# A block-diagonal kv product, lent PSUM banks and a halved last output in a fused attention and snake-MLP kernel

## The chip, the cores and the metric

The kernel runs on one core of one Trainium2 chip. The metric is device time in microseconds (us), the median of several executions. The *span* is the time from the first to the last instruction in the profile, and the *granted clock* is the share of its full clock that TensorE was given. Engines are named as the profile names them: PE is TensorE (PEld its weight loads), DVE is VectorE, ACT is ScalarE, POOL is GpSimd, SP is SyncE. A line such as L235 is line 235 of that kernel's file, so the same statement has different numbers in different kernels.

## The reference, cut to what matters

```python
# q, k, v: (batch 8, heads 8, seq 576, head_dim 64)
q_s = softmax(q, over head_dim);  k_s = softmax(k, over seq)
kv  = einsum('bhsd,bhse->bhde', k_s, v)          # 64 x 64 for each head
x   = einsum('bhsd,bhde->bhse', q_s, kv)         # transposed and reshaped to (4608, 512)
h   = x @ w_in                                   # (4608, 2048)
g   = h + sin(alpha * h)**2 / alpha
out = g @ w_out                                  # (4608, 512)
```

The two large products are computed for nine tiles of 512 tokens ("passes" 0 to 8). A *projection* is the sixteen 128-row blocks ("slots" 0 to 15) of `h`, four 128x512 matmuls each; an *output* is 16 accumulated 128x512 matmuls for 128 tokens, four of them per tile. Attention of batch b must be done before the projection that uses its tokens.

## The kernel before

A slot's projection goes into an accumulator, a piece of PSUM (the memory that this kernel's matmuls write to; a piece of 128x512 float32 is called a *bank* here). ScalarE takes the sine, the square goes to one of three engines, and VectorE *combines* it into `g`, which frees the accumulator. (Copying an accumulator out of PSUM is called its *eviction*.) Most accumulators come from a pool of four banks, `ps_h`. Some slots use a *lent* accumulator from the pool that serves attention at that time.

```python
def mm_h(t, ni, wide=None):
    if wide and ni % 6 >= 4:            # slots 4, 5, 10, 11 are lent
        hp = wide()
    else:
        hp = ps_h.tile([128, MF], F32, name="hp", tag="h")
    for ki in range(4):                 # "..." marks what is left out, here and below
        nc.tensor.matmul(hp, win[:, ki, ...], xT[:, ki, ...], start=(ki == 0), stop=(ki == 3))
    return hp

def attn_out(b, ii, half, pool, eng):   # x of one batch: four calls, four 64x64 tiles each
    ...
    xp = pool.tile([128, 2, 512], F32, name="xp", tag="a")
    for x in range(2):
        r = slice(64 * x, 64 * x + 64)
        for e in range(2):
            nc.tensor.matmul(xp[64 * e:64 * e + 64, x, 0:n], kt[r, e, ii, :],
                             qT[r, j0:j1, ii, e * 64:(e + 1) * 64], start=True, stop=True)
    ...
    eng(xT[:, ii::2, c0:c0 + n], xp[:, :, 0:n])
```

The pool `ps_e` (two buffers of two banks) serves attention and lends in tiles 0 and 1; then it closes, and the output pool `ps_o` is laid over the same banks.

```python
with tc.tile_pool(name="ps_e", bufs=2, space=PSUM, reuse_waits="tile") as ps_e:
    def lent():
        return ps_e.tile([128, 2, MF], F32, name="hh", tag="a")[:, 0]
    ...                                  # projection 0, attention of batch 1
    for ni in range(nN):                 # projection 1
        h_slot(1, ni, SQ[ni], lag, lent)
        flush(lag, 1)                    # combine of the slot before
    cast_v(2, [GP, GP])
    flush(lag, 0)                        # combine of slot 15
ps_o = ctx.enter_context(tc.tile_pool(name="ps_o", bufs=2, space=PSUM, ...))
...
exp_q(2); exp_k(2)
os = o_stream(1)
take(os, 16)                             # first output of tile 1, and its eviction by VectorE
norm_q(2, [GP, V])                       # q reduction of batch 2, on VectorE
exp_q(3); exp_k(3); ...
q_transpose_dma(2)                       # then kv product of batch 2, then projection 2
```

The softmax here doesn't subtract the row's maximum and nothing guards it: scores larger than these inputs give would overflow.

## Time and profile before

| | before |
|---|---|
| time, median of 3 runs | 299.0 us (298.26 to 299.21) |
| span in the profile | 296.6 us |
| TensorE busy | 278.1 us, 94% |
| first projection matmul | 17.00 us |
| projection 1 starts, ends | 49.9, 63.73 us (one matmul at 49.51, the other 63 from 50.14 after a wait; 49.9 is where a start without the wait would lie) |
| projection 2 starts | 82.1 us (likewise: one matmul at 81.47, then a wait) |
| a pass of the middle (passes 3 to 6) | 30.70 us |
| last eviction starts, span ends | 291.86, 296.6 us |

The first view is the profile page of the kernel before: the busy table, then the rows of TensorE's busy share and of its granted clock over 40 slices of the span (each digit is tenths, 9 is 90% or more).

```profile
PE 278.1 (94%) x1595; PEld 127.0 (43%) x1624; DVE 185.5 (63%) x267; ACT 228.5 (77%) x320; POOL 84.6 (29%) x72
...
PE   1999998999898999999999999999999999999993
...
PEclk9999999999999999999999999999999999999999
```

TensorE bounds the kernel nearly everywhere, and every slice shows 90% or more of its clock. So anything gained must be a TensorE wait or a TensorE instruction. One caution on the clock row: the trace's clock record begins at 9.8 us here, and the row shows 9 before that only because nothing is recorded. In the timeline the fourteen warm-up matmuls show another clock:

```profile
6.29 4.90 PE L281 MATMUL warm<-qe,identb 128*128 128x512 bf16 x14 [1.99 <-ACT qe L111]
```

Most of the first nine (to 9.66 us) start 0.43 us apart, as in the half-clock stretch shown further down (67.40 to 67.83 us in the changed kernel), and the last ones (from 9.95 us) 0.22 us, as at full clock later (181.53 to 181.74 us): by this spacing the kernel starts at half clock, unseen in the row.

The second is the timeline of the kernel before around the end of projection 1, TensorE first, then VectorE. Columns: start (us), duration (us), engine, line, operation, out<-in, tile, count; in brackets the idle time before it and what ended that.

```profile
61.15 2.75 PE L215 MATMUL hp<-xT,win 128*128 128x512 bf16 x12
63.73 7.15 PE L235 MATMUL op<-wout,g 128*128 128x512 bf16 x31
...
66.24 0.75 DVE L231 SCALAR_TENSOR_TENSOR g<-s,inva_sb,hp 128x512 bf16<-128x512 f32 x1 [0.41 <-POOL s L225]
67.47 0.69 DVE L241 COPY o<-op 128x512 f32<-128x512 f32 x1 [0.48 <-PE op L235]
68.08 1.34 DVE L139 TENSOR_REDUCE qs<-qe 128x18 f32<-128x1152 bf16 x1
```

The outputs of tile 1 (L235) follow the projection (L215) without a gap, although the last combine (66.24 to 66.99) is still to come. The first output is done and evicted at 67.47, and batch 2's q reduction follows that eviction on VectorE.

The third is the timeline of one tiled attention product in a middle pass of the kernel before, and of the evictions at the very end.

```profile
182.05 0.30 PE L198 MATMUL xp<-qT,kvb 64*64 64x256 bf16 x4
182.29 0.82 PE L235 MATMUL op<-wout,g 128*128 128x512 bf16 x3
...
291.86 0.68 DVE L247 COPY o<-op 64x512 f32<-64x512 f32 x1 [2.76 <-PE op L235]
...
292.58 0.58 ACT L247 COPY o<-op 64x512 f32<-64x512 f32 x1 [14.04 <-DVE o L247]
```

The four tiles use 0.24 us of TensorE's stream (182.05 to 182.29), plus a gap of 0.10 us before them. The last output is evicted in two halves, one after the other.

The fourth is the tile view of w_in in the kernel before: the issue of its loads, and the time from issue to landing.

```profile
L101 POOL DMA_DIRECT2D win<-in_moe_w_in_dram x4: 756/765/918, 10.2 to 12.5; - x4
...
DMA to landing us min/median/max: 5.5/8.3/11.7
```

The last of four quarters was issued at 12.5 us and landed 11.7 us later, at about 24.2 us.

### The profile page before, as it was taken

The page shows a single profiled execution, that of the slowest core. Times are in us where ns is not written, and L with a number is a line of the kernel's source. Part 1 is how long each engine was busy: PE and PEld are TensorE (multiplying, and loading weights), DVE is VectorE, ACT ScalarE, POOL GpSimd, SP SyncE. Part 2 cuts the span into 40 slices and gives each one's busy share as a digit, 9 for nine tenths or more (in the row PEclk, how much of TensorE's full clock was granted, in tenths as well). Part 3 has the DMA queues.
Part 4 walks back from the last instruction along what each step waited for, and adds up shares of the span by engine and source line. Part 5 has one row for each costly group of instructions (what it writes and reads, how often), then busy time and mean ns, then how long its engine had stood idle before and what let it go on. Part 6 is the DMA issues. An engine that isn't in the chain of part 4 may idle for free.

```text
span 296.6 us, 4313 instructions
## 1 busy us (share of the span) xinstructions
PE 278.1 (94%) x1595; PEld 127.0 (43%) x1624; DVE 185.5 (63%) x267; ACT 228.5 (77%) x320; POOL 84.6 (29%) x72
## 2 busy tenths in 40 slices
PE   1999998999898999999999999999999999999993
PEld 0444454444343444344444444444444444444441
DVE  2858664889648857764786568656874555555420
ACT  4788666999577899779987998799877777777400
POOL 0949453575755635001600052005000000000000
PEclk9999999999999999999999999999999999999999
DMA  7999979966789966109921894113411111111233
GB/s 263 278 206 200 314 266 298 398 245 184 162 135 368 390 203 128 39 6 331 289 53 23 277 291 98 39 35 69 83 35 35 38 35 35 35 39 43 48 86 71
DMA packets 35540, 45.76 MB, mean 154 GB/s; under 512 B 15792, under 2 KB 20416, under 8 KB 35520
## 3 DMA queue, kind: packets, MB, share of 16 engines
q1 hardware_dynamic: 29520, 34.09, 40.8%
q0 software_dynamic: 5888, 11.27, 15.2%
q8 instruction: 12, 0.20, 0.3%
q10 hardware_dynamic: 112, 0.14, 0.2%
q14 instruction: 8, 0.07, 0.1%
HBM read 36.71 MB, written 9.44 MB: 156 GB/s over the span
## 4 chain that ended last, share of the span: by engine, by line
PE 63%; ACT 15%; DVE 8%; DMA 4%; issue 4%; POOL 3%; SPq 1%; ACTq 0%
PE hp L215 28%; PE op L235 24%; ACT s L221 4%; DVE g L231 4%; ACT ke L111 3%; DMA st_v<-in_v_dram 3%; POOL s L225 2%; PE xp L198 2%; PE acc L235 2%; PE kvp L151 2%; PE hp L235 2%; ACT s L223 2%; ACT L221 2%; ACT L111 2%; ACT qe L111 2%
## 5 line engine op out<-in xcount | busy, mean ns | idle before, releaser
L231 DVE SCALAR_TENSOR_TENSOR g<-s,inva_sb,hp 128x512 bf16<-128x512 f32 x132 | 96.8, 745 | 68.5 <-ACT s L223 54.3
L215 PE MATMUL hp<-xT,win 128*128 128x512 bf16 x515 | 130.5, 379 | 2.7 <-DVE g L231 1.2
L235 PE MATMUL op<-wout,g 128*128 128x512 bf16 x498 | 125.7, 379 | 1.2 <-issue 0.6
L221 ACT ACTIVATE s<-hp,alpha_sb 128x512 f32<-128x512 f32 x132 | 88.9, 681 | 30.4 <-PE hp L215 23.2
L215 PEld LDWEIGHTS <-win 128*128 128x128 bf16 x576 | 55.7, 98 | 70.9 <-issue 4.3
L235 PEld LDWEIGHTS <-g 128*128 128x128 bf16 x576 | 54.1, 98 | 65.4 <-DVE g L231 0.4
L223 ACT ACTIVATE s<-s 128x512 f32<-128x512 f32 x112 | 70.5, 630 | 3.7
L141 POOL TENSOR_TENSOR qn<-qe,qs 128x2304 bf16<-128x2304 bf16 (+1 forms) x8 | 26.6, 3330 | 87.2 <-DVE qs L140 81.7
L225 POOL TENSOR_TENSOR s<-s 128x512 f32<-128x512 f32 x28 | 29.5, 1061 | 23.9 <-ACT s L221 23.8
L139 DVE TENSOR_REDUCE qs<-qe 128x18 f32<-128x1152 bf16 (+1 forms) x11 | 20.7, 1882 | 14.3 <-ACT qe L111 14.2
L241 DVE COPY o<-op 128x512 f32<-128x512 f32 x31 | 21.0, 677 | 10.1 <-PE op L235 10.1
L111 ACT ACTIVATE qe<-st_q 128x1152 bf16<-128x1152 f32 x16 | 17.9, 1155 | 4.8 <-DMA st_q<-in_q_dram 4.7
L111 ACT ACTIVATE ke<-st_k 128x1152 bf16<-128x1152 f32 x16 | 17.7, 1150 | 2.6 <-DMA st_k<-in_k_dram 2.6
L201 DVE CAST xT<-xp 128x512 bf16<-128x512 f32 (+1 forms) x24 | 17.8, 747 | 1.9 <-PE xp L198 1.5
L125 POOL CAST vb<-st_v 128x1152 bf16<-128x1152 f32 x14 | 16.1, 1178 | 8.8 <-DMA st_v<-in_v_dram 8.7
L198 PE MATMUL xp<-qT,kvb 64*64 64x256 bf16 (+1 forms) x128 | 9.7, 302 | 2.7 <-DVE xT L201 1.2
L247 ACT COPY o<-op 64x512 f32<-64x512 f32 x1 | 0.6, 581 | 14.0 <-DVE o L247 14.0
L198 PEld LDWEIGHTS <-kvb 64*64 64x64 bf16 x128 | 4.5, 103 | 13.9 <-issue 11.3
L151 PE MATMUL kvp<-vb,ke 64*128 64x130 bf16 x288 | 9.8, 216 | 0.6 <-DVE qT L181 0.6
L111 ACT ACT_TABLE_LOAD x7 | 9.0, 1283 | 1.3 <-PEq L477 1.2
L151 PEld LDWEIGHTS <-ke 64*128 64x128 bf16 x288 | 8.3, 93 | 3.7 <-issue 2.4
L201 ACT CAST xT<-xp 128x640 bf16<-128x640 f32 (+1 forms) x8 | 5.1, 653 | 5.9 <-PE xp L198 5.9
(52 smaller groups left out, 112.3 us busy)
## 6 DMA issues: line engine op xcount, KB each, us to landing
out_dram<-o SPq DMA_DIRECT2D x71, 128.0 KB, 2.4
st_q<-in_q_dram SPq DMA_DIRECT2D x5, 1152.0 KB, 6.8
st_k<-in_k_dram SPq DMA_DIRECT2D x5, 1152.0 KB, 9.3
st_v<-in_v_dram SPq DMA_DIRECT2D x5, 1152.0 KB, 10.4
st_k<-in_k_dram POOLq DMA_DIRECT2D x2, 1152.0 KB, 12.2
win<-in_moe_w_in_dram POOLq DMA_DIRECT2D x4, 512.0 KB, 8.3
wout<-in_moe_w_out_dram POOLq DMA_DIRECT2D x4, 512.0 KB, 16.3
st_q<-in_q_dram SPq DMA_DIRECT2D x2, 576.0 KB, 4.8
```

The source lines that it names most:

```text
L111: nc.scalar.activation(dst[:, :, ii * 128:(ii + 1) * 128].rearrange("p j (x d) -> p x j d", x=2), src[:, ii::2], AX.Exp)
L139: nc.vector.tensor_reduce(part, src, axis=AXL.X, op=ALU.add)
L141: engs[h].tensor_tensor(dst, src, part.unsqueeze(3).to_broadcast([128, J, w, D]), op=ALU.mult)
L151: nc.tensor.matmul(kvp[:, e, ii * 130:(ii + 1) * 130], ke[r, j, ii * 128:(ii + 1) * 128], vt[r, j, ii * 130:(ii + 1) * 130], start=(j == 0 ...
L201: eng(xT[:, ii::2, c0:c0 + n], xp[:, :, 0:n])
L215: nc.tensor.matmul(hp, win[:, ki, ni * 128:(ni + 1) * 128], xT[:, ki, t * MF:(t + 1) * MF], start=(ki == 0), stop=(ki == 3))
L221: nc.scalar.activation(s, hp, AX.Sin, scale=alpha_sb[:, ni:ni + 1])
L223: nc.scalar.activation(s, s, AX.Square)
L225: nc.gpsimd.tensor_tensor(s, s, s, op=ALU.mult)
L231: nc.vector.scalar_tensor_tensor(G[t][:, ni], in0=s, scalar=inva_sb[:, ni:ni + 1], in1=hp, op0=ALU.mult, op1=ALU.add)
L235: nc.tensor.matmul(acc, G[t][:, ni, j * 128:(j + 1) * 128], wout[:, ni, :], start=(ni == 0), stop=(ni == nN - 1))
L241: eng(o, acc)
```

## The change

Its intent has five parts.

1. **Block-diagonal kv.** The two heads' 64x64 kv blocks are written into a 128x128 matrix whose other half stays zero, so the attention product takes two full-array matmuls in place of four tiled ones. Rows of `x` come out in another order, so w_in's rows are loaded to match, from 64-partition transfers, the second half as one pair.
2. **The last w_out chunk** is loaded behind batch 1's inputs, not ahead of them.
3. **Four output accumulators at once** for tile 0 (`o_quad`), on banks that are free early. For this the lent slots move from `ni % 6 >= 4` to `ni % 6 in (2, 3)`.
4. **Some evictions and output matmuls move**, to even out the passes. With them come a fourth output buffer, another choice of engines for the squares of tile 0, and batch 1's loads a slot or two earlier.
5. **The last output is halved**: two halves of 256 columns, the first stored under the second.

```diff
-    win_v = moe_w_in.rearrange("(ko ki) n -> ki ko n", ki=128)
+    win_v = moe_w_in.rearrange("(x c d) n -> x d c n", x=2, c=4)
...
-    def load_win(c):
-        nc.gpsimd.dma_start(out=win[:, :, c * 512:(c + 1) * 512], in_=win_v[:, :, c * 512:(c + 1) * 512])
+    def load_win(c0, c1):
+        n = slice(c0 * 512, c1 * 512)
+        for x in range(2):
+            nc.gpsimd.dma_start(out=win[64 * x:64 * x + 64, :, n], in_=win_v[x][:, :, n])
...
-            nc.vector.tensor_tensor(kt[r, :, i0:i1], src[r, :, :, x, 0:D],
+            nc.vector.tensor_tensor(kt[r, :, i0:i1, r], src[r, :, :, x, 0:D],
...
-        for x in range(2):
-            r = slice(64 * x, 64 * x + 64)
-            for e in range(2):
-                nc.tensor.matmul(xp[64 * e:64 * e + 64, x, 0:n], kt[r, e, ii, :],
-                                 qT[r, j0:j1, ii, e * 64:(e + 1) * 64], start=True, stop=True)
+        for e in range(2):
+            nc.tensor.matmul(xp[:, e, 0:n], kt[:, e, ii], qT[:, j0:j1, ii, e * 64:(e + 1) * 64],
+                             start=True, stop=True)
...
-        if wide and ni % 6 >= 4:
+        if wide and ni % 6 in (2, 3):
...
-        for c in range(4):
-            load_win(c)
-        for c in range(4):
+        for c0, c1 in ((0, 1), (1, 2), (2, 4)):
+            load_win(c0, c1)
+        for c in range(3):
             load_wout(c)
...
+            if ni == 11:
+                load_wout(3)
...
-        take(os, 32)
...
+        accs = [ps_h.tile([128, dm], F32, name="hp", tag="h") for _ in range(4)]
+        os = o_quad(0, accs, [DVE_CP, ACT_CP, DVE_CP, ACT_CP])
+        take(os, 44)
...
-    take(os, 24)
+    take(os, 27)
     for n in range(4):
         attn_out(2, n // 2, n % 2, ps_a, ACT_CP)
-        take(os, (3, 3, 2, 1000)[n])
+        take(os, (2, 1, 1, 1000)[n])
...
-    take(o_stream(nT - 1))
+    take(o_stream(nT - 1), 48)
+    for h in range(2):
+        cols = slice(h * 256, h * 256 + 256)
+        acc = ps_o.tile([128, 256], F32, name="op", tag="o")
+        for ni in range(nN):
+            nc.tensor.matmul(acc, G[nT - 1][:, ni, 384:512], wout[:, ni, cols], start=(ni == 0), stop=(ni == nN - 1))
+        evac_o(nT - 1, 3, acc, DVE_CP, cols, (nc.sync, nc.scalar))
```

## The prediction

> **What bounds the kernel.** TensorE is busy 94% of the 296.6 us span (busy table). In the timeline a 128x512 matmul takes 0.2156 us of the stream (0.862 per four), so the 1152 matmuls of the two products are 248 us. The other 48 us are the head (first projection matmul at 17.0 us), attention matmuls, TensorE waits around batches 1 to 3, and 4.8 us after the last matmul (291.8 us). From 111 to 221 us each pass of 30.7 us is TensorE-bound with one wait of 0.16 to 0.21 us.

> **What it removes.**
> 1. Full-array kv product. Four tiled 64x64 matmuls take 0.34 us (N=256) or 0.36 us (N=320), including a gap of 0.10 us before them. [...] Two full-array matmuls should take 0.22 and 0.27 us (from 0.2156 us per 512 columns): 0.42 us less per batch. With one more output matmul ahead of the second projection slot the 0.16 us wait goes: -0.58 us in each of four passes, -2.4 us.
> 2. Batch 1. Landings (DMA view): q 36.1 and 37.5, k 40.6, v 43.6 us, behind the last w_out chunk (34.7; one chunk is 2.65 us). Now they land 2.7 us earlier and that chunk last, just before its use. TensorE's waits between 44 and 50 us (1.2 us) and at 30.7 us (0.55 us) mostly go.
> 3. Tail. Half of the last output is stored under the other half; one 0.4 us copy replaces 0.68 and 0.58 us in series: -0.85 us.

> **What it adds.**
> - w_in comes as 64-partition transfers, its second half as one pair. Before, the last quarter landed at 24.3 us; the third quarter is wanted at 24.0 us: a stall of 0.3 to 1 us. [...] So stage one gains only about 1.1 us.
> - Lent accumulators move from slots 4,5 to 2,3 of six, so slots 14 and 15 are lent. In the built order the first output matmul after batch 1's projection waits for the last combine (before: 66.24 to 66.99 us) instead of starting at 63.73 us: TensorE idles 3.3 us. VectorE evicts that output before batch 2's q reduction, so the chain reduction, q transpose, kv product, next projection is 3.3 us late too. The three matmuls moved ahead of the kv product only fill a wait.
> - After batch 2's projection the first output matmul waits for combine 14, and two evictions moved to ScalarE make ScalarE the limit: no net gain (+0.1 us).

> **Sum.** -1.1 +3.3 +0.1 -2.4 -0.85 = about -0.95 us; I allow a little more for waits counted twice. Predicted 297.5 us, range 295.0 to 299.3. Faster by over 2%: 0.07; within 2%: 0.90; slower: 0.03.

> **Checks.** (a) The waits view shows TensorE's output matmul waiting about 3 us for VectorE's g at 62 to 66 us. (b) Pass to pass falls from 30.7 to 30.1 us. (c) The first matmul of projection 1 comes near 48.8 us (before 49.5). (d) From last matmul to the end: 3.9 us. (e) A wait for w_in at 24 us under 1 us.

> **What would make it wrong.** 64-partition loads much slower (stall of several us); the wait for the last combine hidden, or the reduction not held by it (then about 294 us); full-array kv matmuls held by their weight loads.

## The result, and the profile after

The changed kernel took 302.86 us (median of 4 runs, 302.55 to 303.2), beside 299.09 us for the kernel before. The ratio is 1.0132, with a 95% interval from 1.0111 to 1.0154. Ratios here are the mean time of one kernel's fast runs over that of the other's of the same rounds, so not quite the ratio of the medians quoted. The kernel is 1.3% slower, where about 0.5% faster was predicted, and the time lies above the predicted range of 295.0 to 299.3 us.

The profile page of the changed kernel, the same lines as of before:

```profile
PE 280.3 (93%) x1548; PEld 133.1 (44%) x1576; DVE 186.5 (62%) x270; ACT 228.3 (76%) x320; POOL 84.6 (28%) x73
...
PE   2999999959979999999999999999999999999994
...
PEclk9999999986999999999999999999999999999999
```

TensorE has 47 recorded matmuls fewer, yet is busy 2.2 us longer. In slice 9 (60.3 to 67.8 us) its busy digit falls to 5, and in slices 9 and 10 the clock row shows 8 and 6, where it was full before. These two rows already hold most of the story: an idle spell, and a lower clock after it.

The waits view of the changed kernel (us in total, times, longest) names the idle spell:

```profile
PE op L235 <- DVE g L231: 3.9, 2, 3.1
...
PE xp L198 <- DVE xT L201: 1.0, 4, 0.3
```

The 3.1 us wait is the one that check (a) of the prediction asked for. The kernel before has no such group. The timeline of the changed kernel at the same place, TensorE and then VectorE:

```profile
61.99 1.89 PE L215 MATMUL hh<-xT,win 128*128 128x512 bf16 x8
67.02 5.70 PE L235 MATMUL op<-wout,g 128*128 128x512 bf16 x13 [3.14 <-DVE g L231]
72.92 3.40 PE L235 MATMUL op<-wout,g 128*128 128x512 bf16 x15 [0.19 <-issue]
...
66.22 0.75 DVE L231 SCALAR_TENSOR_TENSOR g<-s,inva_sb,hh 128x512 bf16<-128x512 f32 x1 [0.41 <-POOL s L225]
73.55 0.69 DVE L241 COPY o<-op 128x512 f32<-128x512 f32 x1 [6.58 <-PE op L235]
74.16 1.34 DVE L142 TENSOR_REDUCE qs<-qe 128x18 f32<-128x1152 bf16 x1
```

Projection 1 ends at the same time as before (63.71 against 63.73 us). The last slots now use lent buffers (`hh`), so the first output matmul waits for the combine of slot 15, as predicted. It starts 3.29 us later than before. But VectorE's eviction of that output comes 6.08 us later (73.55 against 67.47): after the wait the thirteen recorded matmuls alone take 5.70 us, where the kernel before does 31 in 7.15 us.

The windows view shows why. Its columns are the stretch (us), its length, the busy time and count of TensorE, of its weight loads, of VectorE, ScalarE and GpSimd, then the mean granted clock, the DMA share and GB/s. First the kernel before, then the changed kernel:

```profile
63.60:67.00 3.40, 3.35 (x16) 1.39 (x15) 2.89 (x5) 3.34 (x5) 2.63 (x3) 1.00 0.11 37
67.00:69.00 2.00, 2.00 (x11) 0.90 (x11) 1.53 (x2) 2.00 (x3) 1.42 (x2) 1.00 0.00 0
```

```profile
63.60:67.00 3.40, 0.28 (x2) 0.00 (x0) 2.87 (x5) 3.34 (x5) 2.62 (x3) 0.86 0.02 7
67.00:69.00 2.00, 1.98 (x5) 0.69 (x5) 0.00 (x0) 2.00 (x3) 1.39 (x2) 0.50 0.03 8
69.00:71.00 2.00, 2.00 (x6) 0.73 (x5) 0.00 (x0) 2.00 (x3) 0.00 (x0) 0.50 0.00 0
71.00:73.00 2.00, 1.81 (x6) 0.67 (x5) 0.00 (x0) 2.00 (x3) 0.00 (x0) 0.53 0.00 0
```

From 67 to 73 us the granted clock is half, and TensorE does five or six matmuls in 2 us in place of eleven. The same view in stretches of half a microsecond tells when the clock fell and when it came back:

```profile
65.50:66.00 0.50, 0.00 (x0) 0.00 (x0) 0.31 (x1) 0.50 (x1) 0.50 (x1) 1.00 0.00 0
66.00:66.50 0.50, 0.00 (x0) 0.00 (x0) 0.28 (x1) 0.49 (x2) 0.50 (x2) 0.55 0.00 0
...
72.50:73.00 0.50, 0.31 (x2) 0.23 (x2) 0.00 (x0) 0.50 (x2) 0.00 (x0) 0.62 0.00 0
```

Each of these stretches mixes full and half clock. A mean of 0.55 puts the fall at about 66.05 us, and 0.62 the return at about 72.88 us (an estimate from these two means): 6.8 us at half clock, of which the last 5.9 us were used.

The other places, in the timelines of the changed kernel: an attention product in a middle pass, the third product of that pass, the first projection's wait for w_in, and the last eviction.

```profile
218.34 0.38 PE L198 MATMUL xp<-qT,kbd 128*128 128x256 bf16 x2
218.56 0.81 PE L235 MATMUL op<-wout,g 128*128 128x512 bf16 x3
...
222.06 0.38 PE L198 MATMUL xp<-qT,kbd 128*128 128x256 bf16 x2 [0.26 <-DVE xT L201]
...
24.72 1.89 PE L215 MATMUL hh<-xT,win 128*128 128x512 bf16 x8 [0.20 <-DMA win<-in_moe_w_in_dram]
...
297.25 0.42 DVE L241 COPY o<-op 128x256 f32<-128x256 f32 x1 [1.32 <-PE op L468]
```

The product takes 0.22 us of the stream (218.34 to 218.56), against 0.24 plus the gap of 0.10 us before. That is the predicted saving, but the third product now waits 0.26 us for the second one's eviction in each pass.

| place in the profile | before | after | difference |
|---|---|---|---|
| projection 1 ends | 63.73 | 63.71 | 0.0 |
| first output matmul after it | 63.73 | 67.02 | +3.3 |
| that output evicted, q reduction of batch 2 starts | 67.47, 68.08 | 73.55, 74.16 | +6.1 |
| first kv product of batch 2 | 78.11 | 84.81 | +6.7 |
| slot 1 of pass 3 | 105.36 | 112.45 | +7.1 |
| slot 1 of pass 6 | 197.51 | 203.41 | +5.9 |
| last eviction starts | 291.86 | 297.25 | +5.4 |
| span ends | 296.6 | 301.4 | +4.8 |

(All in us from the start of the span; 0.2 us of the row of pass 3 is one output matmul that the change puts ahead of it.) From 6.1 to 6.7 us the q transpose took 5.3 us from issue to landing, not 4.7 us. The kept traces place this 0.6 us without explaining it: the transpose took 4.6 to 4.7 us in the three kernels with the tiled product (before, experiments 2 and 11), also when it came late, and 5.3 us or more in all with the full-array product, experiment 6 included. So it comes with part 1 of the change; why is open.

### The profile page after: what moved, and what is told of

The parts are those of the page before. It is cut to its first block, busy times and chain, and to the rows that moved or that the text cites. A ratio compares the mean times of both kernels' runs of the same rounds, so it can differ in the third digit from the quotient of the medians.

```text
span 301.4 us, 4222 instructions
## 1 busy us (share of the span) xinstructions
PE 280.3 (93%) x1548; PEld 133.1 (44%) x1576; DVE 186.5 (62%) x270; ACT 228.3 (76%) x320; POOL 84.6 (28%) x73
## 4 chain that ended last, share of the span: by engine, by line
PE 72%; DVE 10%; ACT 6%; POOL 4%; issue 3%; DMA 3%; ACTq 0%; SPq 0%; POOLq 0%
PE op L235 31%; PE hp L215 28%; PE hp L235 4%; DVE g L231 3%; POOL s L225 3%; ACT s L221 3%; PE xp L198 3%; PE warm L279 2%; DVE xT L201 2%; PE kvp L154 2%; DMA qT<-qn 2%; ACT s L223 1%; DMA st_q<-in_q_dram 1%; DVE o L241 1%; ACT xT L201 1%
## 5 line engine op out<-in xcount | busy, mean ns | idle before, releaser
L231 DVE SCALAR_TENSOR_TENSOR g<-s,inva_sb,hp 128x512 bf16<-128x512 f32 x126 | 92.3, 746 | 62.6 <-ACT s L223 52.7
L235 PE MATMUL op<-wout,g 128*128 128x512 bf16 x480 | 124.0, 386 | 5.0 <-DVE g L231 3.9
L215 PE MATMUL hp<-xT,win 128*128 128x512 bf16 x495 | 125.9, 379 | 0.8
L221 ACT ACTIVATE s<-hp,alpha_sb 128x512 f32<-128x512 f32 x126 | 85.7, 683 | 27.2 <-PE hp L215 22.8
L223 ACT ACTIVATE s<-s 128x512 f32<-128x512 f32 x112 | 70.5, 630 | 3.5
L241 DVE COPY o<-op 128x512 f32<-128x512 f32 (+1 forms) x33 | 21.9, 663 | 20.3 <-PE op L235 17.9
L201 ACT CAST xT<-xp 128x512 bf16<-128x512 f32 (+1 forms) x10 | 6.3, 637 | 13.2 <-PE xp L198 13.1
L198 PE MATMUL xp<-qT,kbd 128*128 128x256 bf16 (+1 forms) x64 | 12.4, 285 | 4.2 <-ACT xT L201 2.0
L235 PE MATMUL hp<-wout,g 128*128 128x512 bf16 x62 | 15.0, 379 | 0.5 <-DVE g L231 0.3
L198 PEld LDWEIGHTS <-kbd 128*128 128x128 bf16 x64 | 6.0, 97 | 12.7 <-issue 5.9
L215 PE MATMUL hh<-xT,win 128*128 128x512 bf16 x48 | 11.3, 379 | 0.2 <-DMA win<-in_moe_w_in_dram 0.2
```

The costliest lines, as they stand in the source:

```text
L198: nc.tensor.matmul(xp[:, e, 0:n], kt[:, e, ii], qT[:, j0:j1, ii, e * 64:(e + 1) * 64], start=True, stop=True)
L201: eng(xT[:, 2 * ii:2 * ii + 2, c0:c0 + n], xp[:, :, 0:n])
L215: nc.tensor.matmul(hp, win[:, ki, ni * 128:(ni + 1) * 128], xT[:, ki, t * MF:(t + 1) * MF], start=(ki == 0), stop=(ki == 3))
L221: nc.scalar.activation(s, hp, AX.Sin, scale=alpha_sb[:, ni:ni + 1])
L223: nc.scalar.activation(s, s, AX.Square)
L231: nc.vector.scalar_tensor_tensor(G[t][:, ni], in0=s, scalar=inva_sb[:, ni:ni + 1], in1=hp, op0=ALU.mult, op1=ALU.add)
```

## The experiments

The theory after reading the traces was: (T1) lending slots 14 and 15 in tile 1 makes TensorE idle for 3.3 us, this idle spell halves the clock, and both together delay the chain to projection 2. Rivals were: (R1) the full-array product or the w_in loads cost the time; (R2) the delay comes from the order of VectorE's instructions (eviction ahead of the reduction) and not from the clock; (R3) the clock is low there for another reason than the idle spell. Each run is compared with the kernel before, timed in the same rounds (298.57 us in the first group, 298.65 in the second, 298.61 in the third). All kernels gave correct results.

### 1. The changed kernel with slots 4, 5, 10, 11 lent in tile 1

```diff
-        if wide and ni % 6 in (2, 3):
+        if wide and ni % 6 in ((4, 5) if t == 1 else (2, 3)):
```

> The changed kernel with one number altered: in batch 1's projection the lent accumulators go back to slots 4,5 of six (4, 5, 10, 11); batch 0 and 2 keep 2,3. My theory (the loss is the first output matmul waiting for the last combine, 3.3 us, plus the halved clock that follows, 2.7 us, both passed on to the next projection): that wait falls under 0.5 us, no matmul after it runs at 0.427 us, the first kv product of batch 2 comes at about 78 us instead of 84.8 us, and the time is 296.5 to 297.2 us. Rival (the loss comes from the full-array matmuls, the 64-partition loads or a slower q transpose): the time stays above 300 us.

Measured: 297.81 us, ratio 0.9978 (0.9954 to 1.0002). Its timeline and windows view:

```profile
63.51 7.15 PE L235 MATMUL op<-wout,g 128*128 128x512 bf16 x31
...
67.00:69.00 2.00, 2.00 (x11) 0.90 (x10) 1.76 (x2) 2.00 (x3) 1.19 (x2) 1.00 0.00 0
```

Output matmuls follow the projection without a gap (63.51 us), the q reduction comes at 67.85 us, and the clock stays at full (1.00). One expression therefore carries the loss: against the changed kernel the difference of the ratios is 1.0132 - 0.9978 = 1.5%, 4.6 us of time (about 3.6 to 5.6 us, an estimate from the two intervals), and 6.3 us between the two profiled spans (301.4 and 295.1). But the rest of the change gains only 0.7 us (its interval reaches from nothing to 1.4 us; 1.5 us between the profiled spans) where the prediction's terms without this wait gave about 4.2 us.

### 2. The kernel before with slots 2, 3, ... lent in tile 1

```diff
-        if wide and ni % 6 >= 4:
+        if wide and ni % 6 in ((2, 3) if t == 1 else (4, 5)):
```

> The kernel before with one number altered: lent accumulators in slots 2,3 in batch 1's projection only. My theory: this alone brings the whole loss, a wait of about 3.3 us at 63.7 us, a spell of matmuls at 0.427 us, and a time of 305 to 306 us (6 to 7 us over before). Rival (the loss needs the other parts of the change): within 1 us of before.

Measured: 303.46 us, ratio 1.0162 (1.0118 to 1.0206). The same expression alone makes the old kernel slower by about 4.8 us, without full-array products, w_in pairs or anything else of the change. R1 falls as the cause of the loss. The windows view of this kernel:

```profile
67.00:69.00 2.00, 1.92 (x5) 0.71 (x5) 0.03 (x1) 2.00 (x3) 1.46 (x2) 0.52 0.00 0
```

The half clock follows the 3.1 us wait here too, but lasts half as long: by the means of 0.52 and, from 69 to 71 us, 0.62 it falls at about 67.1 us and is full from about 70.5 us (an estimate), 3.4 us against 6.8 us in the changed kernel's trace. The four runs of this kernel spread unusually, from 301.87 to 304.99 us, and go with their mean clock: 0.997 in the fastest, 0.987 in the slowest. Over their spans this is about 1.8 and 7.9 us at half clock in all (an estimate; part of it lies outside this spell, about 2 us in the profiled run by its mean clock of 0.991). So the half-clock time is not fixed by the program, and the fastest run, with less than one spell of 3.4 us, probably had none: it lies 3.3 us above the kernel before, which is the wait alone.

### 3. TensorE kept busy, first try

Fourteen useless matmuls after projection 1, into the unused second bank of the last lent tile.

```diff
+        full = {}
...
-            return ps_e.tile([128, 2, MF], F32, name="hh", tag="a")[:, 0]
+            full["hh"] = ps_e.tile([128, 2, MF], F32, name="hh", tag="a")
+            return full["hh"][:, 0]
...
+        for _ in range(14):
+            nc.tensor.matmul(full["hh"][:, 1], win[:, 0, 0:128], xT[:, 0, MF:2 * MF], start=True, stop=True)
         cast_v(2, [GP, GP])
         flush(lag, 0)
```

> The changed kernel with 14 useless 128x512 matmuls after batch 1's projection, into the unused half of the last lent buffer, so that TensorE waits for the same combine but is not idle. My theory (idle costs 3.3 us, and the halved clock after it another 2.7 us): the first output matmul still starts at about 67 us, but the 16 matmuls after it take 3.45 us and not 5.9 us, and the time is 2.5 to 3.2 us below the changed kernel, about 300.0 us, though it does more work. Rival (the slow matmuls are slow for another cause, such as their weights or operands): no gain, 302.9 us or more.

Measured: 302.13 us, ratio 1.0118 (1.0099 to 1.0138). The design was at fault, as its timeline shows:

```profile
65.16 2.97 PE L385 MATMUL hh<-xT,win 128*128 128x512 bf16 x13 [1.24 <-ACT s L221]
69.26 7.07 PE L235 MATMUL op<-wout,g 128*128 128x512 bf16 x32 [1.13 <-DVE g L231]
```

The bank was unused, but the tile was not free: the useless matmuls waited for slot 15's sine, the combine of slot 15 waited for the useless matmuls, and the outputs began at 69.26 us, not at 67.02 us. The run still says one thing: with two idle spells of 1.24 and 1.13 us in place of one of 3.3 us the clock stayed at 1.00, and 32 matmuls took 7.07 us.

### 4. TensorE kept busy, second try

The same fourteen matmuls into a tile of their own, from `ps_h`.

```diff
+        idle = ps_h.tile([128, MF], F32, name="hp", tag="h")
+        for _ in range(14):
+            nc.tensor.matmul(idle, win[:, 0, 0:128], xT[:, 0, MF:2 * MF], start=True, stop=True)
         cast_v(2, [GP, GP])
         flush(lag, 0)
```

> The keep-busy test again, without its fault: the 14 useless matmuls now write a projection buffer that has long been free, so nothing waits for them and they wait for nothing new. My theory (3.3 us of idle, plus about 2.7 us because the clock is halved after it): the first output matmul starts at about 67.0 us as in the changed kernel, the 16 matmuls after it take 3.45 us, the eviction after them comes near 70.9 us instead of 73.55 us, and the time is 2.3 to 3.0 us below the changed kernel (299.9 to 300.6 us). Rival (these matmuls are slow for another cause): the eviction stays at 73.5 us.

Measured: 300.81 us, ratio 1.0081 (1.0066 to 1.0097). Its timeline, TensorE and then VectorE:

```profile
63.53 3.19 PE L383 MATMUL hp<-xT,win 128*128 128x512 bf16 x14
66.84 7.07 PE L235 MATMUL op<-wout,g 128*128 128x512 bf16 x32
...
70.49 0.69 DVE L241 COPY o<-op 128x512 f32<-128x512 f32 x1 [3.70 <-PE op L235]
```

and its windows view:

```profile
67.00:69.00 2.00, 2.00 (x11) 0.88 (x10) 0.00 (x0) 2.00 (x3) 1.22 (x2) 1.00 0.00 0
```

The outputs start at the same time as in the changed kernel (66.84 against 67.02 us), and the wait for the combine is still there, but filled. The clock stays at 1.00, eleven matmuls fit into 2 us, and the first output is evicted 3.06 us earlier (70.49 against 73.55). Fourteen matmuls that compute nothing make the kernel faster: by 2.05 us of the medians, 1.5 us by the ratios (1.0132 - 1.0081; about 0.7 to 2.3 us, an estimate from the two intervals), and 3.0 us between the profiled spans (298.4 and 301.4). So R3 falls: the idle spell causes the half clock. What remains to experiment 1, 1.0% or 3.1 us, is the wait itself.

The profiled gain is larger than the timed one. The profiled run of the changed kernel was its slowest of four (303.2 us, mean clock 0.989; the others 0.992 or 0.993), so its half-clock spell was longer than theirs: over 301 us a mean of 0.992 or 0.993 is 4.2 to 4.8 us at half clock in all (an estimate), and the profiled run had 6.8 us in this spell alone. No trace of the others was kept. One of the four runs of experiment 4 (301.27 us) also shows a mean clock of 0.994; where its clock was low is not known.

### 5. The reduction ahead of the outputs

```diff
-    take(os, 16)
     norm_q(2, [GP, V])
+    take(os, 16)
```

> The changed kernel, wait and all, with batch 2's q normalisation put ahead of the first output eviction in VectorE's order. If the late eviction is what makes the q chain late: the first reduction starts at about 67.6 us instead of 74.2 us, q's transpose lands some 5 us earlier, and the kv product is then held by TensorE's own backlog, at about 83.6 us instead of 84.8 us; time 1.0 to 1.5 us below the changed kernel (301.4 to 301.9 us). If the chain was not held by it: no change.

Measured: 301.56 us, ratio 1.0105 (1.0092 to 1.0118). The first reduction comes at 67.31 us in place of 74.16, and the q transpose is issued at 74.95 in place of 79.38 us, but the kv product of batch 2 starts at 83.09, only 1.7 us earlier than in the changed kernel (84.81). The timeline shows what it waits for:

```profile
83.09 0.38 PE L198 MATMUL xp<-qT,kbd 128*128 128x256 bf16 x2 [0.82 <-DMA qT<-qn]
```

It is still the transpose, though q is normalised at 72.49 us: SyncE issues the transpose behind the stores of the first output (from 73.11 us) and a load, and it lands only 8.0 us after its issue, not 5.3 us (why is open). But TensorE is at work on outputs until 82.27 us, so a transpose in time would have won at most another 0.8 us. So R2 is part of the path and no more: with VectorE's order taken out most of the loss stays, for TensorE itself lost the time.

### 6. The full-array product alone, in the kernel before

Only the block-diagonal kv, the w_in rows and their loads as in the change; lent slots and all else as before.

```diff
+    kbd = [singles.tile([128, 2, 2, 128], BF16, name=f"kbd{n}") for n in range(2)]
...
+        for e in range(2):
+            nc.tensor.matmul(xp[:, e, 0:n], kt[:, e, ii], qT[:, j0:j1, ii, e * 64:(e + 1) * 64],
+                             start=True, stop=True)
...
+        for c0, c1 in ((0, 1), (1, 2), (2, 4)):
+            load_win(c0, c1)
```

> The kernel before with the block-diagonal kv product alone (with the w_in rows and the loads that it needs). If my cost of it holds: each pass of batches 4 to 7 falls by 0.35 to 0.45 us (30.7 to about 30.3), first projection matmul 0.3 to 0.5 us later than before because the weights now need both halves of the normalised kv; in all -1.0 to -1.5 us, 297.6 to 298.1 us. Rival (full-array matmuls as dear as four tiled ones, because tiles run at once): no gain, 299 to 299.6 us.

Measured: 299.32 us, ratio 1.0021 (0.9997 to 1.0045): no gain. A pass falls only from 30.70 to about 30.6 us. The waits view of this kernel says where the saved stream time went:

```profile
PE xp L197 <- DVE xT L200: 2.3, 6, 1.0
PE hp L214 <- DMA win<-in_moe_w_in_dram: 1.7, 1, 1.7
```

The next attention product waits for the eviction of the one before it (2.3 us in six waits, against 1.2 us in two before), because the single `ps_a` accumulator comes free no sooner. A full-array product streams for a shorter time (0.22 us in the changed kernel, against 0.24 us and the gap of 0.10 us), but its results are there later: where the evicting engine is idle (batch 2), from the first matmul to the start of the eviction are 0.42 us (N=256) and 0.47 us (N=320), against 0.35 and 0.38 us tiled. In the middle passes this latency is not what counts: there the second eviction starts 1.12 us after its product's first matmul (0.90 us before), because VectorE is at a combine and an output eviction first. And the first projection waits 1.7 us for the second half of w_in, issued at 13.0 us and landed 12.5 us later, at 25.5 us.

### 7. Slots 4, 5, 10, 11 lent in all later tiles

```diff
-        if wide and ni % 6 in (2, 3):
+        if wide and ni % 6 in ((2, 3) if t == 0 else (4, 5)):
```

> The changed kernel with slots 4,5 lent in batch 1 and batch 2, 2,3 kept in batch 0 only. If the 0.7 us wait of the first output matmul after batch 2's projection is a net cost: 0.4 to 0.7 us below the kernel with slots 4,5 in batch 1 only, 297.1 to 297.4 us. If that stage is held by VectorE and ScalarE and not by the buffer: the wait moves into the projection and the time stays within 0.2 us of it.

Measured: 297.15 us, ratio 0.9954 (0.994 to 0.9968). It is experiment 1 with the like wait after projection 2 (0.71 us there) taken away too; it is 0.66 us faster, across two groups of runs.

### 8. Experiment 7, with batch 2's attention product in four single banks

```diff
+    def attn_out_banks(b, ii, half, engs):
...
+        for e in range(2):
+            xp = ps_h.tile([128, MF], F32, name="hp", tag="h")
+            nc.tensor.matmul(xp[:, 0:n], kt[:, e, ii], qT[:, j0:j1, ii, e * 64:(e + 1) * 64],
+                             start=True, stop=True)
+            engs[e](xT[:, 2 * ii + e, c0:c0 + n], xp[:, 0:n])
...
-        attn_out(2, n // 2, n % 2, ps_a, ACT_CP)
-        take(os, (2, 1, 1, 1000)[n])
+        attn_out_banks(2, n // 2, n % 2, (ACT_CP, DVE_CP))
+        take(os, (0, 2, 0, 1000)[n])
```

> The kernel of the run before this one, with batch 2's kv product written to four single-bank buffers that are free at that time, and evicted by ScalarE and VectorE in parallel, instead of one after the other through one double buffer. If the chain from q's transpose through four serial evictions (4.2 us in before, 78.1 to 82.3 us) decides when batch 2's projection starts: it starts about 2 us earlier (80.0 to 80.6 us) and the time falls by 1.5 to 2 us, to about 295.3 us. If something else holds the projection, or the stage after it takes the gain back: under 0.5 us.

Measured: 294.85 us, ratio 0.9868 (0.9852 to 0.9884), 2.3 us less than experiment 7. In that one, ScalarE's timeline shows the four evictions in series, each waiting for a product that waits for the eviction before:

```profile
79.23 0.59 ACT L201 CAST xT<-xp 128x512 bf16<-128x512 f32 x1 [2.73 <-PE xp L198]
...
82.60 0.69 ACT L201 CAST xT<-xp 128x640 bf16<-128x640 f32 x1 [0.52 <-PE xp L198]
```

and projection 2 starts 3.8 us after the first product (78.81 to 82.61 us). With four banks and two evicting engines the timelines of ScalarE, VectorE and TensorE show:

```profile
79.74 0.70 ACT L424 CAST xT<-hp 128x256 bf16<-128x256 f32 x2 [2.54 <-PE hp L422]
...
79.85 1.74 DVE L424 CAST xT<-hp 128x256 bf16<-128x256 f32 x4 [0.54 <-PE hp L422]
...
81.50 2.75 PE L215 MATMUL hp<-xT,win 128*128 128x512 bf16 x12
```

The first product is at 79.43 us and projection 2 at 81.50 us, 2.1 us later. So this serial chain, which takes about 4 us in every form with one accumulator (78.11 to 82.1 us before), could be halved. The change had left it as it was.

### 9. Experiment 8, with w_in's second half as two pairs of quarters

```diff
-        for c0, c1 in ((0, 1), (1, 2), (2, 4)):
+        for c0, c1 in ((0, 1), (1, 2), (2, 3), (3, 4)):
```

> The kernel with slots 4,5 in batches 1 and 2 and the single-bank kv product, with w_in's second half loaded as two pairs of quarters instead of one pair of halves, as the kernel before had it. If projection 0's slot 8 waits for the last landing (0.8 and 1.5 us in the two runs before, 0.2 in the changed kernel, whose projection started later): the wait goes, projection 1 starts 0.5 to 1.5 us earlier (about 49.4 us), and the time falls by 0.4 to 1.2 us, to about 294.0 us. If the combines behind it hold that stage: no gain.

Measured: 293.23 us, ratio 0.982 (0.9807 to 0.9834), 1.6 us less than experiment 8 (1.4 us by the ratios, across two groups of runs). The wait for w_in, which was 1.5 us in experiment 8 (0.2 in the changed kernel's trace), is gone, and projection 1 starts at 49.00 us, 1.66 us earlier than in experiment 8 (50.66). Against the kernel before it is 0.9 us, about the gain in stage one that the prediction had put at 1.1 us and that the changed kernel didn't show.

### 10. Experiment 9, with the third and fourth product of a pass one slot later

```diff
-        elif 5 <= n < 9:
-            attn_out(b, (n - 5) // 2, (n - 5) % 2, ps_a, engs[n % 2])
+        elif n in (5, 6, 8, 9):
+            m = (5, 6, 8, 9).index(n)
+            attn_out(b, m // 2, m % 2, ps_a, engs[(m + 1) % 2])
```

> The same, with the third and fourth kv product of each pass put one projection slot later, so that the third no longer waits for VectorE to evict the second (0.26 us in every pass). If that wait is what the four passes lost of my predicted 0.58 us: pass to pass falls from 30.35 to about 30.1 us and the time by a further 0.8 to 1.0 us, to about 293.1 us. If another wait takes its place: under 0.3 us.

Measured: 291.6 us (291.38 to 291.81), ratio 0.9763 (0.975 to 0.9777). This beats both kernels: 2.4% faster than before. A pass takes 29.94 us (30.35 in the changed kernel, 30.70 before), and the waits of a product for VectorE's eviction are gone. Its profile page:

```profile
PE 275.5 (95%) x1548; PEld 132.6 (46%) x1576; DVE 187.2 (65%) x274; ACT 227.3 (78%) x320; POOL 85.3 (29%) x75
...
PE   2999999999999999999999999999999999999994
```

TensorE has the same 1548 recorded matmuls as in the changed kernel, and no slice below 90% between the first and the last.

### 11. The halved last output alone, in the kernel before

The code of `evac_o` and of the last output as in the change, nothing else.

> The kernel before with the halved last output alone. By the trace of the changed kernel the time from the last matmul to the end falls from 4.8 to 4.2 us and the matmuls in two halves cost 0.05 us: -0.5 to -0.6 us, 298.0 to 298.2 us. By my prediction: -0.85 us.

Measured: 297.66 us, ratio 0.9967 (0.9954 to 0.9981): 0.98 us faster (0.57 to 1.37). From the start of the last eviction to the end of the span are 4.13 us, against 4.74 before.

## Why the prediction was wrong

Two steps failed: the price of the idle spell, and the sum of the gains. The first is, in the prediction's words, "TensorE idles 3.3 us. ... so the chain reduction, q transpose, kv product, next projection is 3.3 us late too." The idle spell was right to a tenth of a microsecond (63.71 to 67.02 us), and so were its place and its cause: the last combine frees the bank that the first output needs. What was missed is that the idle spell also halves TensorE's clock (0.50 from 67 to 71 us), in the profiled run for 5.9 us of work. From the first output's first matmul to its eviction are then 6.5 us in place of 3.7 us, and the chain is 6.1 us late at the reduction, not 3.3 us. Experiment 4 isolates this: with the spell filled by useless matmuls the clock stays full (1.00) and 1.5 to 2 us of time come back (3.0 us between the profiled spans).

The prediction priced the spell at its own 3.3 us and nothing behind it. In the traces the clock was 0.50 after the spell, and its half-clock time was 6.8 us in the changed kernel, 3.4 us in experiment 2 and 3.4 us in experiment 5 (66.2 to 69.6 us): it is not the same in every trace. That this is why the times of experiment 2 spread by 3 us fits the runs' mean clocks (about 1.8 to 7.9 us at half clock, an estimate); no trace of the other runs was kept to show it.

The clock was not the whole miss, and in the timed runs not even the larger part. The prediction was 297.5 us and the result 302.86 us, 5.4 us more. By the timed runs, the lent slots cost 4.6 us where 3.3 us were predicted (1.3 us of the miss, with an uncertainty of about 1 us), and the second step that failed, the rest of the change, gained 0.7 us where its terms gave about 4.2 us (3.5 us of the miss). The last 0.6 us is what the prediction took off its own sum "for waits counted twice". By the profiled spans the two steps are about 3.0 us and 2.7 us. Point by point, the rest was:

- **Full-array product in the passes: mis-sized.** "-0.58 us in each of four passes, -2.4 us" came out as 0.35 us, 0.5 us in the first (30.70 to 30.35), 1.5 us in all. The stream time was right (0.22 against 0.34 us with the gap). A gap of 0.10 us stood before the tiled product at 182.05 us, and none before the full-array one at 218.34 us; what makes it was not tested. But the third product now waits 0.26 us for the second's eviction, which VectorE reaches only after a combine and an output eviction. Experiment 10 moves it and gets another 1.6 us.
- **Stage one: mis-sized.** "about 1.1 us" was 0.0 us in the changed kernel's trace: projection 1 starts at 49.90 us as before. The waits at 30.7 and 44 to 50 us mostly went (0.33 us is left of 1.2 us), but others came: the first projection matmul was 0.46 us later (17.46 us; but it lies between 16.8 and 17.6 us in the kernels with the new loads and between 16.73 and 17.37 us in the three with the old ones, so this may be scatter), the w_in pair held it for 0.20 us, and a combine held the outputs for 0.28 us at 34.28 us. Experiment 9 shows the pair's part.
- **w_in: right, but by luck.** A stall "under 1 us" was 0.2 us in the changed kernel, but 0.8 to 1.7 us in experiments 6, 7 and 8 with the same loads: there the first projection matmul came at 16.8 to 16.9 us, in the changed kernel at 17.46 us, so that more of the load was done. The loads as a whole ended little later with 64 partitions: the last transfer landed at 24.5 us (24.3 to 25.5 us in the kernels with these loads), against 24.2 us before. The stall came from waiting for half of w_in at once, and quarters took it away.
- **Batch 2's chain: "no net gain (+0.1 us)" was too kind.** With the lent slots put right in tile 1, slot 1 of pass 3 still comes 0.8 us later than before (106.15 against 105.36 in experiment 1). Of this, 0.2 us is the output matmul put ahead, and 0.71 us is a new wait for a combine, the one that the prediction named but held to be made up for elsewhere. Experiment 7 took this wait out, and experiment 8 another 2.3 us from the serial products before projection 2.
- **Tail: right within the noise.** -0.85 us predicted, 0.98 us measured alone (0.57 to 1.37 us), 0.6 us in the traces of the changed kernel and of experiment 11.
- **Checks.** (a) came true (3.1 us), and so did (e) (0.2 us). (b) was 30.35 us, not 30.1; (c) 49.90 us, not 48.8; (d) 4.2 us, not 3.9 (4.8 before).

Why the q transpose took 0.6 us longer with the full-array product stays open.

## What to carry to other kernels

When PSUM banks pass from one stage's pool to the next, ask which instruction frees them last: lending a stage's last slots made the next stage wait 3.3 us for them, and lending earlier slots showed no such wait. Price a TensorE idle spell like those here (3.3 us) as itself plus a stretch at half clock behind it (3.4 or 6.8 us in the traces here, probably none in one run), and check the clock row of the profile at each such spell before anything else. A product that uses less of TensorE's stream gains little (0.13 us in a pass of 30.70 us, alone) while its accumulator and its eviction are in series; the good parts of this change paid (291.6 us, 2.4% faster than before) only after the banks, the loads and the spacing had been put right one by one.
